# Slot 0 of the second mixture set between the last steps of the states' block, token sums fixed behind their slot, and a second staging buffer for weights

## The chip, the cores and the metric

The kernel runs on one core of a Trainium2 chip. The core has TensorE (PE, matrix products into PSUM), VectorE (DVE), ScalarE (ACT), GpSimd (POOL, here only an issuer of transfers) and SyncE (SP, the other issuer). Each engine works through its own queue in order, and waits by semaphores for the others. The metric is the device time of one execution in microseconds: 1490.43 as the median of three runs (1489.2 to 1496.42).

## The reference, cut to what matters

```
attention:  x (8, 8, 512, 64), state (8, 8, 32, 64), scale 1/8
  a     = softmax(scale * x @ state^T)      xread = a  @ state
  a2    = softmax(scale * state @ x^T)      sread = a2 @ x
  out   = concat([xread, sread], axis=2)    -> 8 x (512 + 32) = 4352 rows of 512
mixture 1 (d_ff 1536):  x = ((x @ w_a) * (x @ w_b)) @ w_out
mixture 2 (d_ff 2048):  h = x @ w_in;  x = (h - tanh(h)) @ w_out
```

All is float32. The kernel writes each operand of a large product as a high and a low part (a rounded copy and what is left), and multiplies hi·hi + hi·lo + lo·hi, so that every product is three matmuls. Weights come as 64-bit floats and are decoded on the chip.

## The kernel before, in words

**Blocks.** The 4352 rows are taken as nine blocks with the model's 512 features on partitions: eight of 512 tokens (one for each batch) and a last one, `blk == NB`, of 256 columns, the states. Attention of a block runs beside the first mixture of the block before.

**First mixture.** A block has `FA = 12` steps, one for each 128 of d_ff. `AB(blk, f)` computes the two products into the PSUM banks p2 and p3 (`pab`); ACT copies the first (`ac`), DVE multiplies it by the second, ACT and DVE split the result into `ph` (L517 to L520). `X1(blk, f - 1)` adds the output product of the step before to the four banks `acc`; after step 11 the banks are copied to `ev` and stored to a buffer `x1d` in memory (L535 to L540).

**Weights of the second mixture.** Beside token blocks 2, 3, 5, 6 and 7, `b_words` decodes the second mixture's weights. For `w_in` it also forms the sums and differences of 256-column pieces that Strassen's scheme (in Winograd's form) needs. Each result is split on ACT and DVE into one staging buffer, `hlb` in the place w22, and POOL stores it to memory: `whd` for `w_in` (two stores for each buffer), `wod` for `w_out`. They are loaded again as `wh` and `wo` when they are used.

**Second mixture.** It runs in slots. A slot `(blk, j)` is one eighth of d_ff for one block; `slots` lists all 72. For a token block, `pair_slot` forms 256 rows of h for 512 columns by seven half-sized products, the *pieces*, each a `part` of six matmuls: the token operands are B11, B21, B22 and the sums T1 to T4, made of the block's `x1r` and `x1s` (two halves of the block, loaded by `xr_load`) in seven stages of `x_stage` (L567 to L575). Products gather in the PSUM tiles px, py and pz; px is copied between its pieces (`snap`, L682, L695, L701, L712) and DVE adds the copies to py and pz to get h (L691, L704, L715). From h, ACT and DVE make g = h − tanh(h) (a polynomial where h is small) with u, t, y, k, then `g` as high and low parts. g of slot s goes into the output product `O` (matmuls `acc<-g,wo`) during slots s + 1 and s + 2. The states' block takes the plain form of the slot.

**What sets the order.** The program is written in one order; a scheduler then places every instruction in its engine's queue, by that order and by when it thinks operands are there. So an instruction can stand well ahead of its place in the program. A pool of buffers gives names in turn; an instruction that fills a buffer waits for the last reader of what was in it. `tc.issue_after(x)` keeps what is inside from being placed ahead of x.

**The passage.** The code from L880 on runs the states' block through its twelve steps; step 3 ends with the load of block 0, steps 5 to 11 each hold one stage of its sums. Slot 0 begins behind that, with the last output product of the states' block (`X1(NB, FA - 1)`) between its first pieces:

```
        if f == 3:
            xr_load(0, 5)
        if 4 < f:
            x_stage(0, f - 5)
...
        if blk < NB:
            pair_slot(s, between=(lambda: X1(NB, FA - 1)) if s == 0 else None)
```

Of the kernel before, what the change touches and what calls it, by code (L numbers as in the profile page):

```python
# [8 lines left out]
F32 = mybir.dt.float32  # L9
# [7 lines left out]
KT = 4  # L17
FA = 12
# [26 lines left out]
def fused_kernel(ctx: ExitStack, tc, xT, xn, stp, stq, wA, wB, outT, outS):  # L45
# [153 lines left out]
    half = slice(0, 256), slice(256, 512)  # L199
    U = {}  # L200

    def keep(src, to):
        hl = w_tile(22, [128, 2, 2, 256], F32R, "hlb")
        s3 = src.rearrange("p (a c) -> p a c", a=2)
        nc.scalar.mul(hl[:, :, 0, :], s3, 2.0 ** -8)  # L205
        nc.vector.scalar_tensor_tensor(hl[:, :, 1, :], s3, 2.0 ** -8, hl[:, :, 0, :].bitcast(F32),  # L206
                                       ALU.mult, ALU.subtract)
        for i, d in enumerate(to):
            nc.gpsimd.dma_start(d, hl[:, i].rearrange("p h c -> p (h c)"))

    def b_words():
        i = BU[0]
        BU[0] += 1
        j, part = divmod(i, 6)
        d = whd[j]
        if part in (0, 1, 4, 5):
            raw = DB.raw.pop(0)
            t = small.get([128, 512], I32, "bt", DT)
            h = raw[:, :, 1]
            nc.scalar.mul(h.bitcast(F32), h.bitcast(F32), 2.0 ** -111)  # L220
            words(t, h, raw)
            DB.done += 1
            if DB.done not in (11, 12):
                DB.load()
            t = t.bitcast(F32)
            if part < 2:
                U[part] = t
                keep(t, [d[:, 1], d[:, 2]] if part == 0 else [d[:, 0], d[:, 7]])
            else:
                f = j + FP * (part - 4)  # L230
                hl = w_tile(22, [128, 2, 512], F32R, "hlb")
# [11 lines left out]
    BU = [0]  # L243

    def wh_load(s, j, nb=False):

# [253 lines left out]
    def AB(blk, f, bg=None, after=None):  # L500
        n = 512 if blk < NB else 256
        a = None
        for s in range(2):
            pt = ab.get([128, 512], F32, "pab")
            if blk < NB:
                m = MM[blk, f].rearrange("p a (g s c) -> p a g s c", g=2, s=2)
                for G in range(2):
                    product(pt, (m[:, 0, G, s, :], m[:, 1, G, s, :]), HL[blk][G], slice(0, n), G == 0, G == 1)
            else:
                for k in range(KT):  # L510
                    product(pt, [w[:, s, k, :] for w in WH[f]], X0S[k], slice(0, n), k == 0, k == KT - 1)
            if s == 0:
                a = small.get([128, 512], F32, "ac", AC)
# [12 lines left out]
    def X1(blk, f):  # L526
# [5 lines left out]
            product(acc[m], pair(WO[f], block(m)), ph, slice(0, n), f == 0, f == FA - 1)  # L532
        if f == FA - 1:
            for m in range(KT):
                e = small.get([128, 512], F32, "ev", AT) if m < 3 else small.get([128, 512], F32, "ev", AC)  # L535
                if m % 2:
                    nc.vector.tensor_copy(e[:, :n], acc[m][:, :n])
                else:
# [14 lines left out]
    def width(s):  # L553
        return 512 if slots[s][0] < NB else 256

    def xr_load(blk, place):
        n = 512 if blk < NB else 256
        raw = [big.get([128, 2, 512], F32, "x1r", XIN), w_tile(place, [128, 2, 512], F32, "x1s")]
        for m in range(KT):
            nc.sync.dma_start(raw[m // 2][:, m % 2, :n], x1d[blk][m])  # L560
        RAWX[blk] = raw
        XB[blk] = {}

    def x_pair(blk, name, i, src):
# [64 lines left out]
        nc.vector.copy_predicated(y, k.bitcast(I32), t)  # L629

    def g_hi(s, g):
        GG[s, g] = big.get([128, 2, 512], F32R, "g", Q[0:3] + mix.names[0:2])
        nc.scalar.copy(GG[s, g][:, 0, : width(s)], EW[s, g][2])  # L633

    def g_lo(s, g):
# [29 lines left out]
        O(s, g, m)  # L665
        evac(s, g, m)

    def pair_slot(s, between=None):
        blk, j = slots[s]
        y_, z_ = (abp.tile([128, 512], F32, tag=t, name=n)[:, half[0]] for t, n in (("p0", "py"), ("p2", "pz")))  # L670
# [5 lines left out]
        if between:  # L676
            between()
        if s:
            dve_rest(s - 1, 0)
            act_ut(s - 1, 1)  # L680
# [12 lines left out]
            dve_rest(s - 1, 1)  # L693
        part(x_, s, 3, "T2", False, True)
        nc.scalar.copy(sn[:, 1], x_)  # L695
        part(z_, s, 4, "T3", True, True)
        OE(s - 2, 1, 2)
        part(x_, s, 5, "T1", False, True)
        nxt = border.index(blk) + 1
        stage = {0: 0}.get(j, j - 1 if j > 1 else None)  # L700
        nc.scalar.copy(sn[:, 2], x_)  # L701
        if s:
            g_hi(s - 1, 1)
        nc.vector.tensor_tensor(h2[:, half[1]], sn[:, 2], z_, ALU.add)  # L704
        if s:
            g_lo(s - 1, 1)
        OE(s - 2, 1, 3)
        O(s - 1, 0, 0)
        if stage is not None and nxt < len(border):
            x_stage(border[nxt], stage)  # L710
        part(x_, s, 6, "B22", False, True)
        nc.scalar.copy(h1[:, half[1]], x_)  # L712
        O(s - 1, 0, 1)
        part(z_, s, 7, "T4", False, True)
        nc.vector.tensor_tensor(h2[:, half[0]], sn[:, 1], z_, ALU.add)  # L715
# [161 lines left out]
                t()  # L877


    for f in range(FA):  # L880
        AB(NB, f)
# [6 lines left out]
        if f > 0:  # L888
            X1(NB, f - 1)
        else:  # L890
            X1(NB - 1, FA - 1)
        if f >= 4 and 2 * f - 1 in OPL:
            wo_load(OPL.index(2 * f - 1))
        if f == 3:
            xr_load(0, 5)
        if 4 < f:
            x_stage(0, f - 5)

    last = len(slots) - 1
    for s, (blk, j) in enumerate(slots):  # L900
        if j == 0 and blk < NB:
            xr_load(blk + 1, 21)
        if blk < NB:
            pair_slot(s, between=(lambda: X1(NB, FA - 1)) if s == 0 else None)
        else:
            plain_slot(s)
        if s < last - 1:
# [54 lines left out]
```

## Time and profile before

| | |
|---|---|
| median of three runs | 1490.43 us (1489.2 to 1496.42) |
| the profiled execution | 1493.69 us |
| its span, first to last instruction | 1491.6 us |
| mean granted clock of TensorE, share of full | 0.995 |
| busy PE, PE weight loads, DVE, ACT, POOL | 98%, 82%, 75%, 60%, 11% |
| chain that ended last | PE 80%, DMA 8%, DVE 6%, issue 4%, ACT 2% |

The span is the time between the first and the last instruction; the profiled execution's own time has some 2 us around it. Matmuls are pipelined and their ends are modelled, so PE counts as busy also when it works slowly: the clock stands beside it. The granted clock has two levels here, 2.4 GHz (1.00) and 1.2 GHz (0.50); a stretch with both shows their mean. Along the time, the first 60 us hold the start, attention and first mixture run to about 690 us, the states' block to about 753 us, the second mixture to the end.

### The profile page before, as it was taken

The page shows a single profiled execution, that of the slowest core. Times are in us where ns is not written, and L with a number is a line of the kernel's source. Part 1 is how long each engine was busy: PE and PEld are TensorE (multiplying, and loading weights), DVE is VectorE, ACT ScalarE, POOL GpSimd, SP SyncE. Part 2 cuts the span into 40 slices and gives each one's busy share as a digit, 9 for nine tenths or more (in the row PEclk, how much of TensorE's full clock was granted, in tenths as well). Part 3 has the DMA queues.
Part 4 walks back from the last instruction along what each step waited for, and adds up shares of the span by engine and source line. Part 5 has one row for each costly group of instructions (what it writes and reads, how often), then busy time and mean ns, then how long its engine had stood idle before and what let it go on. Part 6 is the DMA issues. An engine that isn't in the chain of part 4 may idle for free.

```text
span 1491.6 us, 23237 instructions
## 1 busy us (share of the span) xinstructions
PE 1461.5 (98%) x8660; PEld 1225.8 (82%) x8660; DVE 1122.7 (75%) x1969; ACT 894.6 (60%) x1721; POOL 168.6 (11%) x318
## 2 busy tenths in 40 slices
PE   6999999999999999999899999999999999999999
PEld 3776777777888777788888888888888889888998
DVE  6986645777543768674378989889898988888887
ACT  5764445555443555453266867777676777777665
POOL 0000001222000222220210000000000010001010
PEclk9999999999999999999999999999999999999999
DMA  8733435676456576753875655756565665756544
GB/s 288 244 124 115 151 125 188 214 222 209 128 138 178 160 242 212 224 188 116 264 228 176 223 177 175 227 177 223 179 224 177 185 218 170 219 169 205 170 142 127
DMA packets 102624, 280.44 MB, mean 188 GB/s; under 512 B 14064, under 2 KB 43248, under 8 KB 92784
## 3 DMA queue, kind: packets, MB, share of 16 engines
q0 software_dynamic: 40320, 178.28, 39.2%
q1 hardware_dynamic: 62192, 100.68, 20.4%
q8 instruction: 68, 1.11, 0.3%
q14 instruction: 44, 0.36, 0.1%
HBM read 216.53 MB, written 62.39 MB: 187 GB/s over the span
## 4 chain that ended last, share of the span: by engine, by line
PE 80%; DMA 8%; DVE 6%; issue 4%; ACT 2%; POOL 1%; SPq 0%; ACTq 0%; POOLq 0%; DVEq 0%
PE acc L417 37%; PE pab L417 13%; PE px L598 12%; PE pz L598 6%; DMA whd<-hlb 4%; PE py L598 3%; PE mq L471 3%; PE mp L430 2%; DMA wod<-hlb 1%; DVE hlb L206 1%; ACT hlb L205 1%; DMA x1s<-x1d 1%; PE sc L292 1%; DVE ph L520 1%; PE pr L367 1%
## 5 line engine op out<-in xcount | busy, mean ns | idle before, releaser
L417 PE MATMUL acc<-g,wo 128*128 128x512 f32 (+1 forms) x1728 | 438.2, 386 | 0.1
L417 PEld LDWEIGHTS acc<-g,wo 128*128 128x128 f32 x1728 | 293.0, 190 | 42.9 <-DVE g L638 2.4
L417 PE MATMUL acc<-ph,wo 128*128 128x512 f32 (+1 forms) x1296 | 307.8, 385 | 7.7 <-DVE ph L520 4.8
L417 PE MATMUL pab<-hl,mx 128*128 128x512 f32 x1152 | 294.6, 403 | 1.5 <-ACT ac L514 1.5
L417 PEld LDWEIGHTS acc<-ph,wo 128*128 128x128 f32 x1296 | 232.8, 189 | 61.0 <-DVE ph L520 5.5
L417 PEld LDWEIGHTS pab<-hl,mx 128*128 128x128 f32 x1152 | 212.5, 189 | 63.8 <-issue 9.1
L249 POOL DMA_DIRECT2D wh<-whd x144 | 76.2, 529 | 678.7 <-PE pz L598 608.3
L517 DVE TENSOR_TENSOR ac<-ac,pab 128x512 f32<-128x512 f32 (+1 forms) x108 | 70.5, 652 | 109.3 <-PE pab L417 108.3
L633 ACT CAST g<-y 128x512 fp32r<-128x512 f32 (+1 forms) x144 | 85.7, 595 | 89.8 <-DVE y L629 89.1
L598 PEld LDWEIGHTS px<-T,wh 128*128 128x128 f32 x768 | 108.3, 190 | 15.4 <-ACT snap L695 2.6
L598 PE MATMUL px<-T,wh 128*128 128x256 f32 x768 | 114.7, 286 | 3.4 <-ACT snap L695 1.8
L638 DVE TENSOR_TENSOR g<-y,g 128x512 fp32r<-128x512 f32 (+1 forms) x144 | 95.1, 660 | 26.9 <-ACT g L633 26.9
L598 PE MATMUL px<-B,wh 128*128 128x256 f32 x768 | 115.1, 285 | 0.0
L598 PE MATMUL pz<-T,wh 128*128 128x256 f32 x768 | 114.7, 283 | 0.0
L598 PEld LDWEIGHTS pz<-T,wh 128*128 128x128 f32 x768 | 106.8, 190 | 6.9
L598 PEld LDWEIGHTS px<-B,wh 128*128 128x128 f32 x768 | 106.3, 192 | 6.7 <-ACT snap L701 0.5
L622 DVE SCALAR_TENSOR_TENSOR y<-y,u 128x512 f32<-128x512 f32 (+1 forms) x144 | 95.0, 660 | 20.0 <-ACT y L614 18.9
L629 DVE COPY_PREDICATED y<-k,t 128x512 f32<-128x512 int32 (+1 forms) x144 | 104.4, 725 | 2.1
L514 ACT COPY ac<-pab 128x512 f32<-128x512 f32 (+1 forms) x108 | 60.1, 557 | 72.5 <-PE pab L417 70.9
L618 ACT ACTIVATE k<-u,consts 128x512 f32<-128x512 f32 (+1 forms) x144 | 99.8, 693 | 0.0
L623 DVE SCALAR_TENSOR_TENSOR u<-t,u 128x512 f32<-128x512 f32 (+1 forms) x144 | 94.3, 655 | 7.1 <-ACT k L618 1.0
L614 ACT ACTIVATE y<-u,consts 128x512 f32<-128x512 f32 (+1 forms) x144 | 99.0, 688 | 0.7 <-DVE g L638 0.6
(234 smaller groups left out, 2059.2 us busy)
## 6 DMA issues: line engine op xcount, KB each, us to landing
wh<-whd POOLq DMA_DIRECT2D x64, 1024.0 KB, 5.3
wh<-whd POOLq DMA_DIRECT2D x72, 768.0 KB, 4.6
ml<-md POOLq DMA_DIRECT2D x72, 256.0 KB, 3.3
raw<-in_wB SPq DMA_DIRECT2D x32, 512.0 KB, 4.6
whd<-hlb POOLq DMA_DIRECT2D x64, 256.0 KB, 3.1
rawab<-in_wA SPq DMA_DIRECT2D x12, 1024.0 KB, 5.4
md<-mst SPq DMA_DIRECT2D x48, 256.0 KB, 2.5
x1d<-ev SPq DMA_DIRECT2D x32, 256.0 KB, 3.8
```

Source lines behind the costliest of these rows:

```text
L249: nc.gpsimd.dma_start(t.rearrange("p a h c -> p a (h c)"), whd[j][:, a:b])
L417: nc.tensor.matmul(dst[:, cols], w[a], x[:, c, cols], start=first and i == 0, stop=last and i == 2)
L514: nc.scalar.copy(a[:, :n], pt[:, :n])
L517: at_v = nc.vector.tensor_tensor(a[:, :n], a[:, :n], pt[:, :n], ALU.mult)
L598: nc.tensor.matmul(dst, WP[s, piece][:, a, block(k)], XB[slots[s][0]][x][:, c, k, :], start=first and k == 0 and i == 0, stop=last and k = ...
L614: nc.scalar.activation(y, u, AF.Square, bias=consts[:, 0:1], scale=1.0)
L618: nc.scalar.activation(k, u, AF.Relu, bias=consts[:, 1:2], scale=1.0)
L622: nc.vector.scalar_tensor_tensor(y, y, PK, u, ALU.add, ALU.mult)
L623: nc.vector.scalar_tensor_tensor(u, t, C3, u, ALU.mult, ALU.mult)
L629: nc.vector.copy_predicated(y, k.bitcast(I32), t)
L633: nc.scalar.copy(GG[s, g][:, 0, : width(s)], EW[s, g][2])
L638: nc.vector.tensor_tensor(gt[:, 1, :n], EW.pop((s, g))[2], gt[:, 0, :n].bitcast(F32), ALU.subtract)
```

## The change

The edit has four parts.

- `stage()` gives the staging buffer of the weights: by turns the place w22 and a place m3 out of `mix`, which at other times holds the states' `sq` and the slots' `snap`.
- Slot 0 is taken out of the loop over slots. `pair_slot` becomes a generator that stops (`yield`) at five points, and the loop over the steps of the states' block drives it during steps 9, 10 and 11. Its pz lies in bank p0, since p2 and p3 are in use by `pab`. Block 0 is loaded in halves behind steps 1 and 3, its seven stages follow the products of steps 4 to 7, and the last output product of the states' block moves behind the first two pieces of slot 1.
- In the states' block `ac` and the four `ev` go to the two RAW places q4 and q5 (`ev` had five places in AT and AC, `ac` two in AC), so that the places of u, t, y, k are free for slot 0. The turn of the places for `g` begins at q2.
- `x_stage` in a slot is held behind the third copy of px and the sum that reads it (`issue_after`). In block 0 the stages of block 1 lie in slots 1 to 7, in later blocks in slots 0 and 2 to 7.

```
--- before.py
+++ after.py
@@ -199,8 +199,15 @@
     half = slice(0, 256), slice(256, 512)
     U = {}
 
+    def stage():
+
+        BU[1] += 1
+        if BU[1] % 2:
+            return w_tile(22, [128, 2, 512], F32R, "hlb")
+        return mix.get([128, 2, 512], F32R, "hlb", SQ)
+
     def keep(src, to):
-        hl = w_tile(22, [128, 2, 2, 256], F32R, "hlb")
+        hl = stage().rearrange("p h (a c) -> p (h a c)", a=2).rearrange("p (a h c) -> p a h c", a=2, h=2)
         s3 = src.rearrange("p (a c) -> p a c", a=2)
         nc.scalar.mul(hl[:, :, 0, :], s3, 2.0 ** -8)
         nc.vector.scalar_tensor_tensor(hl[:, :, 1, :], s3, 2.0 ** -8, hl[:, :, 0, :].bitcast(F32),
@@ -228,7 +235,7 @@
                 keep(t, [d[:, 1], d[:, 2]] if part == 0 else [d[:, 0], d[:, 7]])
             else:
                 f = j + FP * (part - 4)
-                hl = w_tile(22, [128, 2, 512], F32R, "hlb")
+                hl = stage()
                 split(hl, t)
                 nc.gpsimd.dma_start(wod[f], flat(hl))
         elif part == 2:
@@ -240,7 +247,7 @@
             nc.vector.tensor_tensor(U[0][:, half[1]], U[0][:, half[1]], U[0][:, half[0]], ALU.subtract)
             keep(U[0], [d[:, 3], d[:, 6]])
 
-    BU = [0]
+    BU = [0, 0]
 
     def wh_load(s, j, nb=False):
 
@@ -510,7 +517,7 @@
                 for k in range(KT):
                     product(pt, [w[:, s, k, :] for w in WH[f]], X0S[k], slice(0, n), k == 0, k == KT - 1)
             if s == 0:
-                a = small.get([128, 512], F32, "ac", AC)
+                a = small.get([128, 512], F32, "ac", AC) if blk < NB else big.get([128, 512], F32, "ac", RAW)
                 nc.scalar.copy(a[:, :n], pt[:, :n])
         if bg:
             bg()
@@ -532,7 +539,10 @@
             product(acc[m], pair(WO[f], block(m)), ph, slice(0, n), f == 0, f == FA - 1)
         if f == FA - 1:
             for m in range(KT):
-                e = small.get([128, 512], F32, "ev", AT) if m < 3 else small.get([128, 512], F32, "ev", AC)
+                if blk == NB:
+                    e = big.get([128, 512], F32, "ev", RAW)
+                else:
+                    e = small.get([128, 512], F32, "ev", AT if m < 3 else AC)
                 if m % 2:
                     nc.vector.tensor_copy(e[:, :n], acc[m][:, :n])
                 else:
@@ -553,12 +563,13 @@
     def width(s):
         return 512 if slots[s][0] < NB else 256
 
-    def xr_load(blk, place):
+    def xr_load(blk, place, parts=(0, 1)):
         n = 512 if blk < NB else 256
-        raw = [big.get([128, 2, 512], F32, "x1r", XIN), w_tile(place, [128, 2, 512], F32, "x1s")]
-        for m in range(KT):
-            nc.sync.dma_start(raw[m // 2][:, m % 2, :n], x1d[blk][m])
-        RAWX[blk] = raw
+        for i in parts:
+            t = w_tile(place, [128, 2, 512], F32, "x1s") if i else big.get([128, 2, 512], F32, "x1r", XIN)
+            for m in range(2):
+                nc.sync.dma_start(t[:, m, :n], x1d[blk][2 * i + m])
+            RAWX.setdefault(blk, []).append(t)
         XB[blk] = {}
 
     def x_pair(blk, name, i, src):
@@ -629,7 +640,7 @@
         nc.vector.copy_predicated(y, k.bitcast(I32), t)
 
     def g_hi(s, g):
-        GG[s, g] = big.get([128, 2, 512], F32R, "g", Q[0:3] + mix.names[0:2])
+        GG[s, g] = big.get([128, 2, 512], F32R, "g", Q[2:3] + mix.names[0:2] + Q[0:2])
         nc.scalar.copy(GG[s, g][:, 0, : width(s)], EW[s, g][2])
 
     def g_lo(s, g):
@@ -665,16 +676,16 @@
         O(s, g, m)
         evac(s, g, m)
 
-    def pair_slot(s, between=None):
+    def pair_slot(s):
+
         blk, j = slots[s]
-        y_, z_ = (abp.tile([128, 512], F32, tag=t, name=n)[:, half[0]] for t, n in (("p0", "py"), ("p2", "pz")))
+        y_ = abp.tile([128, 512], F32, tag="p0", name="py")[:, half[0]]
         x_ = abp.tile([128, 512], F32, tag=f"p{1 + 2 * (s % 2)}", name="px")[:, half[0]]
         sn = mix.get([128, 3, 256], F32, "snap", SQ)
         h1, h2 = (mix.get([128, 512], F32, "h", [nm]) for nm in (mix.names[2], "ml2"))
         part(y_, s, 2, "B21", True, True)
         part(x_, s, 1, "B11", True, True)
-        if between:
-            between()
+        yield
         if s:
             dve_rest(s - 1, 0)
             act_ut(s - 1, 1)
@@ -693,23 +704,28 @@
             dve_rest(s - 1, 1)
         part(x_, s, 3, "T2", False, True)
         nc.scalar.copy(sn[:, 1], x_)
+        z_ = abp.tile([128, 512], F32, tag="p2" if s else "p0", name="pz")[:, half[0]]
         part(z_, s, 4, "T3", True, True)
+        yield
         OE(s - 2, 1, 2)
         part(x_, s, 5, "T1", False, True)
+        yield
         nxt = border.index(blk) + 1
-        stage = {0: 0}.get(j, j - 1 if j > 1 else None)
-        nc.scalar.copy(sn[:, 2], x_)
+        stage = j - 1 if j > 1 or blk == 0 else (0, None)[j]
+        at_s = nc.scalar.copy(sn[:, 2], x_)
         if s:
             g_hi(s - 1, 1)
-        nc.vector.tensor_tensor(h2[:, half[1]], sn[:, 2], z_, ALU.add)
+        at_v = nc.vector.tensor_tensor(h2[:, half[1]], sn[:, 2], z_, ALU.add)
         if s:
             g_lo(s - 1, 1)
         OE(s - 2, 1, 3)
         O(s - 1, 0, 0)
-        if stage is not None and nxt < len(border):
-            x_stage(border[nxt], stage)
+        if stage not in (None, -1) and nxt < len(border):
+            with tc.issue_after(at_s.ins), tc.issue_after(at_v.ins):
+                x_stage(border[nxt], stage)
         part(x_, s, 6, "B22", False, True)
         nc.scalar.copy(h1[:, half[1]], x_)
+        yield
         O(s - 1, 0, 1)
         part(z_, s, 7, "T4", False, True)
         nc.vector.tensor_tensor(h2[:, half[0]], sn[:, 1], z_, ALU.add)
@@ -877,31 +893,39 @@
                 t()
 
 
+
+    slot = pair_slot(0)
     for f in range(FA):
-        AB(NB, f)
+        stages = {4: (0,), 5: (1, 2), 6: (3, 4), 7: (5, 6)}.get(f, ())
+        AB(NB, f, after=lambda: [x_stage(0, i) for i in stages])
         if f == 0:
             wo_load(0)
         if f in (3, 7):
             wh_load(f // 4, f // 4)
         if f >= 4 and 2 * f - 2 in OPL:
             wo_load(OPL.index(2 * f - 2))
-        if f > 0:
-            X1(NB, f - 1)
-        else:
-            X1(NB - 1, FA - 1)
+        if f >= 9:
+            next(slot, None)
+        X1(*((NB, f - 1) if f else (NB - 1, FA - 1)))
+        if f in (9, 10):
+            next(slot)
         if f >= 4 and 2 * f - 1 in OPL:
             wo_load(OPL.index(2 * f - 1))
-        if f == 3:
-            xr_load(0, 5)
-        if 4 < f:
-            x_stage(0, f - 5)
+        if f in (1, 3):
+            xr_load(0, 5, (f // 2,))
+    xr_load(1, 21)
+    wh_load(2, slots[2][1])
 
     last = len(slots) - 1
     for s, (blk, j) in enumerate(slots):
+        if s == 0:
+            continue
         if j == 0 and blk < NB:
             xr_load(blk + 1, 21)
         if blk < NB:
-            pair_slot(s, between=(lambda: X1(NB, FA - 1)) if s == 0 else None)
+            for i, _ in enumerate(pair_slot(s)):
+                if s == 1 and i == 0:
+                    X1(NB, FA - 1)
         else:
             plain_slot(s)
         if s < last - 1:
```

How the queues stand. First DVE in the states' block before, between the `ph` of two steps (ac and ph are the product and its low part; L575 is a subtraction among the token sums, x1r the first half of a block's load):

```order
L520 TENSOR_TENSOR ph<-ac,ph 128x256
L569 TENSOR_TENSOR T_6975<-x1s,T_6975 128x512
L517 TENSOR_TENSOR ac<-ac,pab 128x256
L575 TENSOR_TENSOR x1r<-x1r 128x2x256
L520 TENSOR_TENSOR ph<-ac,ph 128x256
L517 TENSOR_TENSOR ac<-ac,pab 128x256
```

The same queue in the change, around the stages of steps 6 and 7:

```order
L524 TENSOR_TENSOR ac<-ac,pab 128x256
L586 TENSOR_TENSOR x1r<-x1s,x1r 128x2x256
L527 TENSOR_TENSOR ph<-ac,ph 128x256
L580 TENSOR_TENSOR T_6707<-x1r,T_6707 128x512
L580 TENSOR_TENSOR T_6711<-x1s,T_6711 128x512
L524 TENSOR_TENSOR ac<-ac,pab 128x256
L527 TENSOR_TENSOR ph<-ac,ph 128x256
```

The subtraction for block 1 no longer stands among the steps of the states' block; the sums of block 0 stand behind `ph` of their step.

PE at the end of the states' block before (acc<-ph is the output product of a step, px, py and pz are pieces of slots; wo_1061 and wo_1114 belong to steps 10 and 11):

```order
L417 MATMUL acc<-ph,wo_1061 128x256 x12
L598 MATMUL py<-B_6771,wh_6545 128x256 x6
L598 MATMUL px<-B_6663,wh_6545 128x256 x6
L417 MATMUL acc<-ph,wo_1114 128x256 x12
L598 MATMUL px<-T_6875,wh_6545 128x256 x6
L598 MATMUL pz<-T_6926,wh_6545 128x256 x6
L598 MATMUL px<-T_6823,wh_6547 128x256 x6
L598 MATMUL py<-B_6771,wh_6751 128x256 x4
L598 MATMUL px<-B_6715,wh_6547 128x256 x6
```

And in the change, from output 10 on (wh_6550 is slot 0, wh_6768 and wh_6770 are slot 1, acc<-g the token outputs of slot 0):

```order
L609 MATMUL pz<-T_6765,wh_6550 128x256 x6
L424 MATMUL acc<-ph,wo_1061 128x256 x12
L609 MATMUL py<-B_6655,wh_6768 128x256 x6
L609 MATMUL px<-B_6599,wh_6768 128x256 x6
L424 MATMUL acc<-ph,wo_1114 128x256 x12
L609 MATMUL px<-T_6711,wh_6768 128x256 x6
L609 MATMUL pz<-T_6762,wh_6768 128x256 x6
L609 MATMUL px<-T_6707,wh_6770 128x256 x6
L424 MATMUL acc<-g,wo_0_6395 128x512 x3
L609 MATMUL px<-B_6651,wh_6770 128x256 x6
L424 MATMUL acc<-g,wo_0_6395 128x512 x3
L609 MATMUL pz<-T_6765,wh_6770 128x256 x6
```

Slot 0 is through before output 10, and slot 1 stands where slot 0 stood, with token outputs between its pieces.

ACT in the change at the same place (u, t, y, k of slot 0's second half, then two of the four `ev` among the px copies of slot 1):

```order
L620 ACTIVATE u<-h 128x512
L621 ACTIVATE t<-h 128x512
L625 ACTIVATE y<-u,consts 128x512
L629 ACTIVATE k<-u,consts 128x512
L549 COPY ev<-acc 128x256
L693 COPY snap<-px 128x256
L644 CAST g<-y 128x512
L706 COPY snap<-px 128x256
L549 COPY ev<-acc 128x256
L715 COPY snap<-px 128x256
L578 CAST B_7144<-x1r 128x512
```

Before, the two copies `ev<-acc` stood together behind the first px copy of slot 0.

## Rows read from the trace of the kernel before

**Rows 1.** The page, busy time of each engine (us, share, instructions).
```profile
PE 1461.5 (98%) x8660; PEld 1225.8 (82%) x8660; DVE 1122.7 (75%) x1969; ACT 894.6 (60%) x1721; POOL 168.6 (11%) x318
```

**Rows 2.** Stretches: busy us of each engine (instructions), granted clock, DMA share, GB/s.
```profile
630.00:640.00 10.00, 8.81 (x31) 7.06 (x32) 8.63 (x15) 4.93 (x9) 2.88 (x5) 0.83 0.64 215
...
720.00:730.00 10.00, 5.61 (x45) 5.40 (x44) 2.56 (x6) 0.98 (x3) 2.12 (x4) 0.85 1.02 346
730.00:740.00 10.00, 10.00 (x72) 10.00 (x71) 1.27 (x3) 1.36 (x4) 1.58 (x3) 0.81 0.54 162
...
760.00:770.00 10.00, 7.92 (x42) 6.80 (x41) 9.00 (x16) 7.63 (x16) 0.60 (x2) 0.83 0.67 208
...
800.00:1490.00 690.00, 688.04 (x4329) 618.75 (x4327) 602.58 (x1064) 494.64 (x995) 69.32 (x131) 1.00 0.61 188
```

**Rows 3.** Timeline of PE: start, us, line, operation, out<-in, count [idle before <-releaser].
```profile
710.50 1.58 PE L417 MATMUL acc<-ph,wo 128*128 128x256 f32 x12
...
729.49 2.72 PE L417 MATMUL acc<-ph,wo 128*128 128x256 f32 x11 [4.39 <-DVE ph L520]
...
770.44 0.88 PE L598 MATMUL pz<-T,wh 128*128 128x256 f32 x6
...
823.79 0.88 PE L598 MATMUL py<-B,wh 128*128 128x256 f32 x6
...
825.23 1.57 PE L417 MATMUL acc<-g,wo 128*128 128x512 f32 x6
826.63 0.88 PE L598 MATMUL px<-T,wh 128*128 128x256 f32 x6
```

**Rows 4.** Timeline of DVE, same columns: the passage, and a later slot.
```profile
728.41 0.69 DVE L575 TENSOR_TENSOR x1r<-x1r 128x512 f32<-128x512 f32 x1 [7.20 <-DMA x1r<-x1d]
...
821.00 0.69 DVE L638 TENSOR_TENSOR g<-y,g 128x512 fp32r<-128x512 f32 x1 [0.39 <-ACT g L633]
822.59 0.42 DVE L715 TENSOR_TENSOR h<-snap,pz 128x256 f32<-128x256 f32 x1 [0.89 <-PE pz L598]
823.37 0.69 DVE L622 SCALAR_TENSOR_TENSOR y<-y,u 128x512 f32<-128x512 f32 x1 [0.36 <-ACT y L614]
```

**Rows 5.** Chain of work that ended last, 700 to 775 us: start, us, what.
```profile
703.48 2.88 PE pab L417 x24
...
706.36 1.43 PE acc L417 x12
...
708.17 6.03 DMA x1s<-x1d
```

**Rows 6.** Waits of ACT, 240 to 690 us: total us, times, longest.
```profile
ACT hlb L205 <- DMA whd<-hlb: 57.2, 19, 5.4
```

**Rows 7.** Timeline of ACT: the token blocks' last part, and slots 0 and 1.
```profile
617.44 0.63 ACT L205 ACTIVATE hlb<-bt 128x512 fp32r<-128x512 f32 x1 [5.35 <-DMA whd<-hlb]
...
751.99 0.37 ACT L539 COPY ev<-acc 128x256 f32<-128x256 f32 x1
...
758.62 0.63 ACT L609 ACTIVATE u<-h 128x512 f32<-128x512 f32 x1
...
760.91 0.61 ACT L609 ACTIVATE u<-h 128x512 f32<-128x512 f32 x1
```

**Rows 8.** Waits of PE, 240 to 690 us: total us, times, longest.
```profile
PE acc L417 <- DVE ev L537: 2.6, 2, 1.9
PE pab L417 <- ACT ac L514: 1.5, 2, 1.1
PE pt L303 <- ACT S L350: 1.4, 2, 0.8
```

**Rows 9.** The tile hlb: from issue to landing of its stores.
```profile
DMA to landing us min/median/max: 2.3/3.1/6.2
```

**Rows 10.** DMA issues: count, KB each, median us to landing.
```profile
x1d<-ev SPq DMA_DIRECT2D x4, 128.0 KB, 2.5
```

**Rows 11.** The buffer x1d in memory: from issue to landing, all sizes.
```profile
DMA to landing us min/median/max: 2.0/4.2/8.0
```

More of the change, by code (lines that the diff above doesn't have):

```diff
@@ L200, in fused_kernel, with stage @@
     U = {}
+    def stage():
+        BU[1] += 1
+        if BU[1] % 2:
+            return w_tile(22, [128, 2, 512], F32R, "hlb")
+        return mix.get([128, 2, 512], F32R, "hlb", SQ)
     def keep(src, to):
-        hl = w_tile(22, [128, 2, 2, 256], F32R, "hlb")
+        hl = stage().rearrange("p h (a c) -> p (h a c)", a=2).rearrange("p (a h c) -> p a h c", a=2, h=2)
         s3 = src.rearrange("p (a c) -> p a c", a=2)
@@ L230, in b_words @@
                 f = j + FP * (part - 4)
-                hl = w_tile(22, [128, 2, 512], F32R, "hlb")
+                hl = stage()
                 split(hl, t)
@@ L534, in X1 @@
             for m in range(KT):
[L535 removed]
+                if blk == NB:
+                    e = big.get([128, 512], F32, "ev", RAW)
+                else:
+                    e = small.get([128, 512], F32, "ev", AT if m < 3 else AC)
                 if m % 2:
@@ L554, in width, with xr_load @@
         return 512 if slots[s][0] < NB else 256
-    def xr_load(blk, place):
+    def xr_load(blk, place, parts=(0, 1)):
         n = 512 if blk < NB else 256
[L558 to L561, printed above, removed]
+        for i in parts:
+            t = w_tile(place, [128, 2, 512], F32, "x1s") if i else big.get([128, 2, 512], F32, "x1r", XIN)
+            for m in range(2):
+                nc.sync.dma_start(t[:, m, :n], x1d[blk][2 * i + m])
+            RAWX.setdefault(blk, []).append(t)
         XB[blk] = {}
@@ L666, in OE, with pair_slot @@
         evac(s, g, m)
-    def pair_slot(s, between=None):
+    def pair_slot(s):
         blk, j = slots[s]
-        y_, z_ = (abp.tile([128, 512], F32, tag=t, name=n)[:, half[0]] for t, n in (("p0", "py"), ("p2", "pz")))
+        y_ = abp.tile([128, 512], F32, tag="p0", name="py")[:, half[0]]
         x_ = abp.tile([128, 512], F32, tag=f"p{1 + 2 * (s % 2)}", name="px")[:, half[0]]
@@ L675, in pair_slot @@
         part(x_, s, 1, "B11", True, True)
-        if between:
-            between()
+        yield
         if s:
@@ L695, in pair_slot @@
         nc.scalar.copy(sn[:, 1], x_)
+        z_ = abp.tile([128, 512], F32, tag="p2" if s else "p0", name="pz")[:, half[0]]
         part(z_, s, 4, "T3", True, True)
+        yield
         OE(s - 2, 1, 2)
         part(x_, s, 5, "T1", False, True)
+        yield
         nxt = border.index(blk) + 1
-        stage = {0: 0}.get(j, j - 1 if j > 1 else None)
-        nc.scalar.copy(sn[:, 2], x_)
+        stage = j - 1 if j > 1 or blk == 0 else (0, None)[j]
+        at_s = nc.scalar.copy(sn[:, 2], x_)
         if s:
             g_hi(s - 1, 1)
-        nc.vector.tensor_tensor(h2[:, half[1]], sn[:, 2], z_, ALU.add)
+        at_v = nc.vector.tensor_tensor(h2[:, half[1]], sn[:, 2], z_, ALU.add)
         if s:
@@ L708, in pair_slot @@
         O(s - 1, 0, 0)
-        if stage is not None and nxt < len(border):
-            x_stage(border[nxt], stage)
+        if stage not in (None, -1) and nxt < len(border):
+            with tc.issue_after(at_s.ins), tc.issue_after(at_v.ins):
+                x_stage(border[nxt], stage)
         part(x_, s, 6, "B22", False, True)
         nc.scalar.copy(h1[:, half[1]], x_)
+        yield
         O(s - 1, 0, 1)
@@ L877, in fused_kernel @@
                 t()
+    slot = pair_slot(0)
     for f in range(FA):
-        AB(NB, f)
+        stages = {4: (0,), 5: (1, 2), 6: (3, 4), 7: (5, 6)}.get(f, ())
+        AB(NB, f, after=lambda: [x_stage(0, i) for i in stages])
         if f == 0:
@@ L887, in fused_kernel @@
             wo_load(OPL.index(2 * f - 2))
[L888 to L891, printed above, removed]
+        if f >= 9:
+            next(slot, None)
+        X1(*((NB, f - 1) if f else (NB - 1, FA - 1)))
+        if f in (9, 10):
+            next(slot)
         if f >= 4 and 2 * f - 1 in OPL:
             wo_load(OPL.index(2 * f - 1))
[L894 to L897, printed above, removed]
+        if f in (1, 3):
+            xr_load(0, 5, (f // 2,))
+    xr_load(1, 21)
+    wh_load(2, slots[2][1])
     last = len(slots) - 1
     for s, (blk, j) in enumerate(slots):
+        if s == 0:
+            continue
         if j == 0 and blk < NB:
@@ L903, in fused_kernel @@
         if blk < NB:
-            pair_slot(s, between=(lambda: X1(NB, FA - 1)) if s == 0 else None)
+            for i, _ in enumerate(pair_slot(s)):
+                if s == 1 and i == 0:
+                    X1(NB, FA - 1)
         else:
```

6 lines of the change are left out of this document (3 added, 3 removed).

## The prediction

> **What bounds the kernel now.** I read the page first: TensorE (PE) has matmuls for 98% of the span [rows 1], so only time in which PE stands still or runs slowly can be won. The table of stretches shows where that is. From 800 us to the end PE is idle for 690 − 688.04 = 1.96 us in all, so the second mixture, once it runs, has nothing to give [rows 2]. The losses lie in two places.
>
> The first is the passage from the states' block into the second mixture, 710 to 771 us. The timeline of PE shows a stop of 4.39 us before 729.49, put down to the product `ph` of VectorE (DVE) [rows 3]. The timeline of DVE shows the reason: a subtraction for the *second* block's token sums (L575) stood ahead of `ph` in DVE's queue and waited 7.20 us for its load x1r [rows 4]. The granted clock falls during the stop, and again later: 0.85, 0.81 and 0.83 over the windows 720 to 730, 730 to 740 and 760 to 770 [rows 2], that is 3.0 + 3.8 + 3.4 = 10.2 us at the lower of the two levels, 1.2 GHz.
>
> What the passage loses is best told by its work. One step of the states' block is 24 matmuls of the two products (2.88 us, all 24 in the chain's row) and 12 of the output (1.41) [rows 5]; two of the seven pieces of a slot are 825.23 − 823.79 = 1.44, one is 0.72, and 6 token matmuls are 826.63 − 825.23 = 1.40 [rows 3]. Between the start of the output of step 3 (710.50) and the end of the T4 piece of slot 1 (770.44 + 0.72 = 771.16) PE did 7 x 2.88 + 9 x 1.41 of the states' block, the 14 pieces of slots 0 and 1 and 7 matmuls ahead out of slot 2 (15.17 x 0.72), and 12 token matmuls (2.80): 20.2 + 12.7 + 10.9 + 2.8 = 46.6 us of work in 60.7. **14.1 us** are lost there.
>
> By PE's busy column the loss would be smaller: 4.39 us idle in 720 to 730, none in 730 to 740, 2.08 in 760 to 770 [rows 2], 6.5 in all. The Trainium skill ("Perfetto Trace Analysis", Identifying the Most-Contended Engine) says that matmul busy share is no good measure for TensorE. The trace agrees: 730 to 740 is 10.00 us busy at a clock of 0.81. By the busy column the passage could give 6.5 us, by its work 14.1.
>
> The second place is the preparation of the second mixture's weights beside the token blocks. ScalarE (ACT) waits there 57.2 us, in 19 waits, for the store of the one staging buffer `hlb` [rows 6], up to 5.35 us at a time [rows 7], and its copies out of PSUM stand behind it. PE feels four of these waits: 2.6 us in two through `ev` and 1.5 in two through `ac` [rows 8]. Around the last of them the clock is 0.83 over 10 us [rows 2]: 3.4 us at 1.2 GHz, 1.7 lost. Together **5.8 us**.
>
> **The change part by part.** *Two staging buffers.* The store of a buffer lands 2.3 to 6.2 us after its issue, median 3.1 [rows 9]. A step of a token block has 24 matmuls of 512 columns, 24 x 1.40/6 = 5.6 us [rows 3], and one buffer is filled in a step. With the second buffer ACT returns to a buffer after two steps, 11.2 us, so even the slowest store is in. I take 5.8 us. It adds no instruction. Bounds: 0, if ACT then waits for something as late; a little below nothing, −1.4, if ACT's shifted order doubles the wait of `pt` on `S`, which the change doesn't touch [rows 8]; above, 5.8.
>
> *Slot 0 between steps 9 to 11, the sums of block 0 in steps 4 to 7.* The matmuls are the same. I laid out PE's new order by hand from 710.50 with the durations above. To the end of the products of step 9: 5 x 1.41 + 5 x 2.88, 732.0. From there two pieces, output 8, T2 and T3, products 10, T1, output 9, B22, products 11, T4, output 10, two pieces of slot 1, output 11: 9 x 0.72 + 4 x 1.41 + 2 x 2.88 = 17.9, end 749.8. Then T2, T3, T1, three token matmuls, B22, three, T4, six: 5 x 0.72 + 2.8 = 6.4, end 756.2 without a wait. Against it stands 771.16 less the 7 matmuls of slot 2 (0.84): 770.3.
>
> T3 of slot 0 now shares a bank of PSUM with py and waits for the sum that reads it; output 8 (1.41) lies between and covers the copy (0.37 [rows 7]) and the sum. Two waits are new. (a) PE's T2 of slot 1 needs the copy of px, and ACT has it behind u, t, y, k of slot 0's second half, which begin when T4's sum is there, on DVE behind the last `ph`, at about 747. The four take 760.91 − 758.62 = 2.29 us, the `ev` and the px copy after them 0.37 each [rows 7]: px is out at 750.1 to 750.4, and PE waits 0.5. (b) `ev` of the states' block has two buffers in place of four. The third `ev` waits on ACT for the first one's store, and behind it on ACT is the third copy of px, on which B22 waits; the fourth does the same on DVE, with T4 behind its sum. The first `ev` ends at 749.8; four such stores landed a median of 2.5 us after issue [rows 10], so the third `ev` starts at 752.3 and px is out at 753.1, when PE has just come to B22 (749.8 + 0.5 + 2.16 + 0.70 = 753.2). I put down 0.5 us for what passes between engines. Transfers to and from that memory at large took 2.0 to 8.0 [rows 11]; with 2.0 the wait is gone, with 8.0 it is 757.8 + 0.7 − 753.2 = 5.3. I take the 2.5, as it is the same store. So the end is 756.2 + 1.0 = 757.2 and the passage gains **13.1 us**, between 14.1 (no wait) and 14.1 − 0.5 − 5.3 − 1.7 (one more spell at 1.2 GHz like that after the `ev` stop) = 6.6.
>
> Block 0's second load x1s doesn't move: 6.03 us from 708.17 [rows 5], in at 714.2. The order now puts its first reader behind `ph` of step 5, whose products end at 710.50 + 1.41 + 2.88 = 714.8, so it costs nothing. The loads of block 1 and the weights of slot 2 go out earlier on SP and POOL; what stands behind them there, the last weights of the second mixture, is read by slots much later.
>
> *Token sums behind their slot.* No instruction more, but a fixed place: one cast on ACT and up to two DVE instructions (some 1.3 us) in each of 51 slots, after the third px copy and its sum, where before they were bunched early in a block. In a slot without them DVE has three waits of 0.39, 0.89 and 0.36 us just there, 1.64 in all [rows 4], and the `g` that comes later by it is ready at 821.7 and first read at 825.23 [rows 3]. So it fits: nothing. Bounds: 1.96 us gained [rows 2]; lost, up to the instructions' own time, see the last rival.
>
> **The sum.** 13.1 + 5.8 = 18.9 us from the profiled execution's 1493.69 (span 1491.6 and 2.1 around it): 1474.8. The median of the runs, 1490.43, is 3.3 below that execution, so I predict 1490.43 − 18.9 = 1471.5, **1472 us**.
>
> **The rivals.** *The store of the first `ev` decides* (ACT and DVE at the end of the states' block). For it: SP issues it just after the loads of block 1, and landings up to 8.0 are in the trace. Against: the median of this very store. At 8.0 us with a spell at 1.2 GHz the passage gains 6.6: 1478.0. *The staging gains nothing.* For it: the stores get slower, or ACT's stop is only handed to the next late operand. Against it: 11.2 us for at most 6.2. The gain is 13.1: 1477.3. The Trainium skill ("SBUF — State Buffer", SBUF: two separate sides) warns that a transfer issued by POOL gets no descriptors while DVE runs an instruction that takes both read ports. By that rule these stores land later the busier DVE gets, and a second buffer would only move the wait; the landings reach 6.2 us, twice the median, but no row says in which mode DVE ran. *Slower: the pinned sums hold up each slot.* If DVE can't use its idle time because a sum's operand or the next px copy comes in its middle, `g` and h of each slot come late and PE waits in 51 slots. At 18.9/51 = 0.37 us a slot the gain is gone, from 0.52 the kernel is slower by more than 0.5%; at 0.63, one ACT instruction over 512 columns [rows 7], it costs 32 us, 1504. Against it: 1.64 us idle for 1.3 of work, and 3.5 us between `g` and its reader.
>
> **How the numbers follow.** Forecast 0.64, late store 0.17, staging without gain 0.13, slower 0.04, and 0.02 for pinned sums that eat between half and all of the gain. The lowest time that the bounds allow is 1490.4 − 14.1 − 5.8 − 2.0 = 1468.5; the runs here lie down to 1.2 below their median, so 1467. Upward, the first two rivals together give 1483.8; I stop at 1482 and leave out the slow case. A measurement of this kernel can tell some 0.5%, 7.5 us, from no change: faster means below 1483. The forecast and nearly all of the first two rivals are: faster 0.90; the worst of them and half-eaten gains: same 0.07; slower 0.03.
>
> **What would show it.** Right: no stop of PE above 1 us between 710 and 760, T4 of slot 1 done near 757, the granted clock 1.00 in both places, next to no wait of ACT for stores of `hlb`, 800 us to the end unchanged in length. Wrong: a wait of ACT of several us for a store at the third `ev`; waits of PE on `g` or px copies that recur in every slot; ACT's stops before `hlb` still there with another releaser.

## The result, and the profile after

The changed kernel took 1471.15 us (median of four runs, 1470.33 to 1472.2). The kernel before, on the same chip, took 1491.95 (four runs, 1489.2 to 1496.42). The ratio is 0.9858 with a 95% interval of [0.9831, 0.9885]. The forecast was 1472. The profiled execution took 1472.2 us, with a span of 1470.4, 21.2 less than before.

The page, first the busy time of each engine, then the shares of the chain that ended last:

```profile
PE 1451.6 (99%) x8660; PEld 1223.9 (83%) x8660; DVE 1128.3 (77%) x1969; ACT 904.4 (62%) x1721; POOL 167.6 (11%) x318
...
PE 96%; DMA 1%; DVE 1%; ACT 1%; issue 0%; SPq 0%; ACTq 0%; DVEq 0%
```

The chain has become PE's: 96% after 80%. PE's busy time fell by 1461.5 − 1451.6 = 9.9 us [rows 1] and its idle time by the other 11.3. So nearly half of the gain was time in which PE counted as busy and worked slowly or with small gaps, and the idle time alone doesn't tell the loss. I take it as in the prediction, by its work: for every matmul, the distance to the start of the next one over the usual distance for its shape, summed by stretch (times of the kernel before):

| stretch | lost before | lost after | gain | forecast |
|---|---|---|---|---|
| start, to 60 us | 16.8 | 16.4 | 0.4 | 0 |
| token blocks, 240 to 690 | 12.7 | 4.5 | 8.2 | 5.8 |
| passage, 690 to 800 | 14.1 | 4.4 | 9.7 | 13.1 |
| second mixture, from 800 | 3.3 | 0.4 | 2.9 | 0 |

The sum is 21.2, the difference of the spans (from 60 to 240 us both kernels lose the same); 18.9 were forecast. Three of the four terms missed by 2.4 to 3.4 us, and the misses nearly cancel. The same stretches as in [rows 2], in the changed kernel:

```profile
630.00:640.00 10.00, 10.00 (x44) 8.08 (x44) 7.25 (x13) 4.82 (x9) 2.63 (x5) 1.00 0.63 217
...
720.00:730.00 10.00, 10.00 (x86) 10.00 (x85) 1.69 (x4) 2.30 (x6) 2.50 (x5) 1.00 1.00 351
730.00:740.00 10.00, 10.00 (x86) 10.00 (x86) 5.05 (x11) 5.60 (x12) 2.12 (x4) 1.00 0.85 272
740.00:750.00 10.00, 7.15 (x45) 6.48 (x44) 7.25 (x14) 4.86 (x12) 0.53 (x1) 0.87 0.88 284
750.00:760.00 10.00, 10.00 (x62) 8.97 (x62) 8.26 (x15) 6.39 (x14) 1.06 (x2) 0.96 0.41 111
```

At 630 and at 720 to 740 the clock is 1.00 and PE has work throughout: 86 matmuls in 720 to 730 where there were 45. One loss is left, at 740 to 760. The timeline of PE there (columns as in [rows 3]), then ACT, then the queue of SP:

```profile
742.99 0.89 PE L609 MATMUL px<-T,wh 128*128 128x256 f32 x6
743.72 0.85 PE L424 MATMUL acc<-g,wo 128*128 128x512 f32 x3
747.42 1.65 PE L609 MATMUL px<-B,wh 128*128 128x256 f32 x6 [2.85 <-ACT snap L715]
748.87 1.48 PE L424 MATMUL acc<-g,wo 128*128 128x512 f32 x3
750.15 1.15 PE L609 MATMUL pz<-T,wh 128*128 128x256 f32 x6
```

```profile
740.79 0.35 ACT L549 COPY ev<-acc 128x256 f32<-128x256 f32 x1
...
742.48 0.37 ACT L706 COPY snap<-px 128x256 f32<-128x256 f32 x1 [0.54 <-PE px L609]
746.72 0.37 ACT L549 COPY ev<-acc 128x256 f32<-128x256 f32 x1 [3.87 <-DMA x1d<-ev]
746.99 0.38 ACT L715 COPY snap<-px 128x256 f32<-128x256 f32 x1
```

```profile
738.84 0.80 SPq L571 DMA_DIRECT2D x1s<-x1d  x2
741.17 7.24 SPq L550 DMA_DIRECT2D x1d<-ev  x4
```

This is wait (b) of the prediction. The first `ev` ends at 741.14; the third, in the same buffer, starts 5.58 us later, when the store has landed; behind it stands the third px copy, and for that PE waits 2.85 us before B22. Then 12 matmuls start at the lower clock, the first piece taking 1.65 instead of 0.88: (0.13 + 0.04) x 10 = 1.7 us at full speed lost by the two windows.

ACT's waits in 240:690 (total us, times, longest), the longest group and the two longest before `hlb`, and then the landing of `hlb`:

```profile
ACT ac L521 <- PE pab L424: 47.5, 42, 2.8
...
ACT hlb L212 <- issue: 12.1, 7, 1.8
ACT hlb L212 <- DVE bt L243: 10.4, 8, 1.3
```

```profile
DMA to landing us min/median/max: 2.3/3.8/6.6
```

The 57.2 us of [rows 6] are gone altogether, and so are 18.3 us in eight waits for the stores to `wod` that those rows leave out, though the stores land later than before (median 3.8, 3.1 in [rows 9]): two steps of 5.6 us still cover the longest.

The second mixture's gain is in no wait of PE. The starts of `py`, the first piece of a slot, over a block's edge in the kernel before, and in the changed one:

```profile
834.43 0.88 PE L598 MATMUL py<-B,wh 128*128 128x256 f32 x6
845.20 0.88 PE L598 MATMUL py<-B,wh 128*128 128x256 f32 x6
856.08 0.88 PE L598 MATMUL py<-B,wh 128*128 128x256 f32 x6
866.88 0.88 PE L598 MATMUL py<-B,wh 128*128 128x256 f32 x6
877.52 0.88 PE L598 MATMUL py<-B,wh 128*128 128x256 f32 x6
```

```profile
816.38 0.88 PE L609 MATMUL py<-B,wh 128*128 128x256 f32 x6
827.01 0.88 PE L609 MATMUL py<-B,wh 128*128 128x256 f32 x6
837.65 0.88 PE L609 MATMUL py<-B,wh 128*128 128x256 f32 x6
848.29 0.88 PE L609 MATMUL py<-B,wh 128*128 128x256 f32 x6
```

Before, three slots at each block's edge took 10.77, 10.88 and 10.80 us, the others 10.64; after, all take 10.64. What stretched them stands in the waits of the *weight loads* (PEld), 800:1490, before and then after:

```profile
PEld acc L417 <- DVE g L638: 2.4, 7, 0.4
PEld acc L417 <- ACT g L633: 1.3, 6, 0.2
```

```profile
PEld acc L424 <- DVE g L649: 0.3, 1, 0.3
```

Where the sums were bunched, early in a block, `g` came late: 3.7 us in 13 waits, 0.3 now. They are too short to show as idle time of a pipelined PE.

### The profile page after: what moved, and what is told of

It is laid out like the page before. It is cut to its first block, busy times and chain, and to the rows that moved or that the text cites. A ratio compares the mean times of both kernels' runs of the same rounds, so it can differ in the third digit from the quotient of the medians.

```text
span 1470.4 us, 23250 instructions
## 1 busy us (share of the span) xinstructions
PE 1451.6 (99%) x8660; PEld 1223.9 (83%) x8660; DVE 1128.3 (77%) x1969; ACT 904.4 (62%) x1721; POOL 167.6 (11%) x318
## 4 chain that ended last, share of the span: by engine, by line
PE 96%; DMA 1%; DVE 1%; ACT 1%; issue 0%; SPq 0%; ACTq 0%; DVEq 0%
PE acc L424 45%; PE pab L424 21%; PE px L609 12%; PE pz L609 6%; PE py L609 3%; PE mq L478 3%; PE mp L437 2%; PE pr L374 1%; PE sc L299 1%; DMA x1d<-ev 1%; DMA rawab<-in_wA 1%; PE pt L310 0%; PE mp L443 0%; PE pa L310 0%; DVE sm L324 0%
```

## The experiments

Two questions were open: what made the store behind wait (b) late, and which part of the change earned what. Edits marked "after" start from the changed kernel, "before" from the other. The kernel before ran beside each of them; its medians were 1491.95 to 1492.83, and as the runs are from several chips, a difference of 1 us between two kernels isn't counted.

**The ev wait by more buffers** (after; the four `ev` two to a buffer, so that none waits for a store):

```
 if blk == NB:
-    e = big.get([128, 512], F32, "ev", RAW)
+    if m % 2 == 0:
+        pair_ev = big.get([128, 2, 512], F32, "ev", RAW)
+    e = pair_ev[:, m % 2]
```

> The changed kernel with one edit: the four ev of the states' block lie two to a buffer (as the token blocks' ev do), so that no ev waits for a store. Theory A (the stop of 2.85 us of PE before B22 of slot 1, and the half-speed stretch behind it, come from the third ev's wait for the first one's store): the stop and the low clock at 744 to 751 us go, 3 to 4.4 us less than the changed kernel, 1467 to 1468 us, ratio to before 0.984. Rival (ACT's and DVE's queues are late there anyway, the store is only the last of several): a stop of 2 us or more stays with another releaser, time 1470 to 1471.5.

(The token blocks' `ev` in fact lie one to a buffer; nothing rests on that remark.)

1466.41 us (1465.6 to 1466.89), ratio 0.9827 [0.9807, 0.9848]. The stop is gone, and with it the lower clock:

```profile
740.00:750.00 10.00, 10.00 (x69) 9.00 (x68) 9.79 (x18) 7.50 (x16) 1.05 (x2) 1.00 0.89 302
```

So wait (b) with its spell at the lower clock cost 1471.15 − 1466.41 = 4.7 us, where 0.5 had been put down.

**The ev wait by an earlier landing** (after; still two buffers, but block 1's second load goes out behind the stores; `STORE` keeps the last store of `ev`):

```
-xr_load(1, 21)
+xr_load(1, 21, (0,))
...
 X1(NB, FA - 1)
+with tc.issue_after(STORE[0].ins):
+    xr_load(1, 21, (1,))
```

> The changed kernel with one transfer moved: the second load of block 1 (x1s, 2 x 256 KB) is issued on SP behind the four stores of ev of the states' block, not just ahead of them; the ev keep their two buffers. In the changed kernel SP issues x1s at 738.84 and it lands 7.0 us later (median of two), the first ev's store is issued at 741.17, and the third ev starts at 746.72. Theory Q (the store lands late because it shares its queue and its engines with the 512 KB of x1s just ahead of it): without them it lands in about the 2.5 us of the kernel before; the third ev then waits under 1.0 us on ACT, the stop of PE of 2.85 us falls under 0.6 with no spell at 1.2 GHz behind it, and the time is 1466 to 1467.5, as with the four ev in two buffers (1466.4). Theory G (what is late is the general load of weights, wh and wo on POOL's queue, in flight at the same time): the store still lands after 4.5 to 6 us, the stop stays at 2 to 3 us and the time at 1470 to 1472. In between (landing 3.5 to 4): both share in it, stop near 1.0 to 1.5, 1467.5 to 1469.5. Neither theory expects a wait on x1s itself, which is first read in slot 2.

1466.59 us (1465.89 to 1467.19), ratio 0.9819 [0.9792, 0.9846]. ACT, then the queue of SP:

```profile
739.98 0.35 ACT L551 COPY ev<-acc 128x256 f32<-128x256 f32 x1
...
742.50 0.38 ACT L551 COPY ev<-acc 128x256 f32<-128x256 f32 x1 [0.46 <-DMA x1d<-ev]
```

```profile
740.36 4.57 SPq L552 DMA_DIRECT2D x1d<-ev  x4
745.02 1.21 SPq L573 DMA_DIRECT2D x1s<-x1d  x2
```

The store is in 2.17 us after the first `ev` ended, the wait is 0.46, and PE doesn't stop. So it was x1s, ahead of the store in SP's queue, that made it late, as theory Q has it. But x1s stood as far ahead of the store in the kernel before. What differs is how long x1s itself took (count, KB each, median us to landing; before, then the change):

```profile
x1s<-x1d SPq DMA_DIRECT2D x2, 256.0 KB, 4.0
```

```profile
x1s<-x1d SPq DMA_DIRECT2D x2, 256.0 KB, 7.0
```

In both kernels the first store landed 0.3 us behind x1s: at 755.1 after 754.8, and at 746.6 after 746.3. Whether the place in the queue made it wait, or the 512 KB more on the same DMA engines, these runs don't separate. Nor is theory G refuted. The 768 KB of weights went out on POOL as before (at 736.99), but the 1024 KB only when the first store had landed; in the change they were under way during the wait (issued at 743.56). And in this run the fourth store of `ev`, issued at 744.61 with no load of SP left ahead of it, took 5.5 us where the three before it had taken 1.7 to 2.1. It landed 0.4 us behind these 1024 KB:

```profile
742.75 0.53 POOL L256 DMA_DIRECT2D wh<-whd  x1 [5.24 <-PE pz L611]
```

```profile
x1d<-ev SPq DMA_DIRECT2D x1, 128.0 KB, 5.5
```

The Trainium skill ("DMA: Bandwidth & Descriptors", Queues, rings and completion order) says that what SP issues goes into one queue, consumed in order on each DMA engine, and that an engine alternates between queues. The trace agrees: a store with x1s ahead in SP's queue landed just behind it, and of two stores with only POOL's weights ahead one took 2.1 us and one 5.5.

**The weights behind the stores as well** (the kernel above, `wh_load(2, ...)` moved into the same `with`).

> As the kernel with x1s issued behind the ev stores, and the weight loads of slot 2 (wh, 1024 and 768 KB on POOL, in the changed kernel at 728.46 and 737.80) written behind them as well. Only the landing of the first ev's store tells here; the time may suffer from weights that come late. Theory Q (x1s ahead in the same queue makes the store late): the store lands as in the kernel with x1s alone moved, 2.2 to 3 us, and these weights change nothing but their own lateness: slot 2, which starts near 750, waits for wh some 0 to 5 us, time 1466 to 1474. Theory G (the weights in flight make it late): here alone the store lands in 2.0 to 3 us, while with x1s alone moved it took 4.5 to 6.

1466.61 us (1466.05 to 1467.8), ratio 0.9821 [0.9791, 0.9851]. The edit moved nothing: holding orders the program, but makes POOL wait for nothing on SP, and POOL's queue stood as before. It repeats the run above, and is no test of its own for the weights, which were never moved.

**Staging alone** (before, with `stage()` as in the change).

> The kernel before with the second staging buffer alone. Theory A (the parts add up; the token blocks gain by this buffer alone what they gained in the changed kernel): ACT's waits for stores of hlb go, PE's stops at 305, 317, 617 and 629 us go; 8 us less than before, about 1484 us; the stop of 4.39 us at 725 us is still there. By the sum of the prediction: 5.8 us less, 1486. Rival (the waits move to another operand): within 1.5 us of before.

1484.84 us (1477.77 to 1485.65), ratio 0.994 [0.9918, 0.9962]: 7.8 us gained against the 1492.65 beside it. The loss in the token blocks falls from 12.7 to 4.0, and the passage keeps its stop; on DVE its cause stands as in [rows 4]:

```profile
717.95 0.69 DVE L582 TENSOR_TENSOR x1r<-x1r 128x512 f32<-128x512 f32 x1 [6.63 <-DMA x1r<-x1d]
```

**One staging buffer** (after, `if BU[1] % 2:` made `if True:`).

> The changed kernel with one staging buffer again, all else kept. Theory A (the parts add up): ACT's waits for stores are back, 57 us in the token blocks, and with them 8 us: 1479 us, 12.5 us less than before. Rival (the passage and the staging share a cause, as by the scheduler's order): 1475 or less, or 1484 or more.

1477.21 us (1473.66 to 1478.85), ratio 0.9897 [0.9872, 0.9922], 6.1 above the changed kernel. Waits of PE in 240:690 (total us, times, longest):

```profile
PE acc L424 <- DVE ev L547: 3.0, 2, 1.9
PE pab L424 <- ACT ac L521: 1.4, 1, 1.4
PE pt L310 <- ACT S L357: 1.0, 2, 0.8
```

All three groups of [rows 8], of which the changed kernel has none, are back, the waits of `pt` on `S` among them, which the prediction had called untouched.

**Holding the token sums alone** (before; slot 0 stays where it was, one staging buffer):

```
-            x_stage(border[nxt], stage)
+            with tc.issue_after(at_s.ins), tc.issue_after(at_v.ins):
+                x_stage(border[nxt], stage)
```

> The kernel before with the token sums held behind the third px copy and its sum (issue_after) and nothing else: slot 0 stays behind the states' block. Theory B (most of the passage's loss came from the subtraction for block 1 that stood ahead of ph on DVE): the stop of 4.39 us goes, with its 3.4 us of clock loss; the second mixture is 3 us faster as in the changed kernel; 8 to 11 us less than before, 1481 to 1484. Theory C (the passage's loss is the chain of px copies, sums, u, t, y, k to g of slots 0 and 1 with nothing to do on PE meanwhile, and only work between the steps fills it): the stop moves into slots 0 and 1, the gain is 3 to 5 us, 1487 to 1489.

1479.38 us (1477.54 to 1482.42), ratio 0.9917 [0.9892, 0.9942]: 13.3 gained, more than expected by either. The waits of PE in the passage (690:800) are now:

```profile
PE px L598 <- ACT t L610: 1.5, 1, 1.5
PE px L598 <- ACT snap L695: 0.5, 1, 0.5
PE acc L417 <- DVE ph L520: 0.4, 1, 0.4
```

The stop of 4.39 us on `ph` is gone, since block 1's subtraction can no longer stand ahead of it; the loss of the passage is 4.2 us after 14.1, and from 800 us on every slot but one takes 10.64. So 9.9 of the 13.3 us lie in the passage, and about 3 in the second mixture.

**Staging and holding, slot 0 not moved** (before, with both edits above).

> The kernel before with the second staging buffer and the held token sums, and without the move of slot 0 (no slot between the steps of the states' block, ev in four buffers). Theory B (the held sums gave most of the passage, staging and sums add up): 13.3 us by the sums as run alone plus 8 by staging, 1492 - 21 = 1470 to 1472, as fast as the changed kernel; so the move as made, with its wait for the store of ev, is worth nothing. Rival (the two overlap, the move is needed): 1475 or more.

1471.5 us (1470.98 to 1474.53), ratio 0.9865 [0.9842, 0.9888]: the changed kernel's time, without the move. The two gains add up: 7.8 + 13.3 = 21.1, measured 1492.62 − 1471.5 = 21.1.

**The change without holding** (after, `x_stage` in a slot without its `with`).

> The changed kernel with the token sums of the slots no longer held behind their px copy; the move of slot 0, its stages and the second staging buffer are kept. Theory B (the holding is what keeps block 1's subtraction away from ph on DVE and makes slots even): the 3 us of the second mixture are lost again, slots at a block's edge take 10.8 us and not 10.64, and DVE waits for x1r or x1s ahead of a sum that PE waits for; 1476 to 1482. Rival (the move alone is enough, as block 1's first load comes 20 us earlier in it): the passage is as in the changed kernel, only the 3 us are lost, 1474.

1478.38 us (1478.08 to 1478.84), ratio 0.9907 [0.9882, 0.9931], as theory B had it. Slots at a block's edge take 10.76 to 10.88 again, and in the passage PE waits 3.3 and 2.6 us for px copies.

**The same with ev in pairs.**

> The same without holding, with the four ev two to a buffer as in the fastest version (1466.4). It tells whether what the move and the holding take away in the passage is the same loss. Rival of B (the move alone is enough): passage free of stops, the second mixture 3 us longer, 1469.5. Theory B (a load of block 1 still stops DVE in front of a sum): a stop of PE of 2 us or more between 735 and 760 us, 1472 to 1476.

1477.41 us (1476.92 to 1478.47), ratio 0.9901 [0.988, 0.9922], 11.0 above the kernel with ev pairs and holding. Its DVE, its ACT and its PE:

```profile
726.21 0.69 DVE L588 TENSOR_TENSOR x1r<-x1r 128x512 f32<-128x512 f32 x1 [6.22 <-DMA x1r<-x1d]
```

```profile
726.98 0.62 ACT L580 CAST T<-x1r 128x512 fp32r<-128x512 f32 x1 [5.10 <-DVE x1r L588]
```

```profile
728.23 0.98 PE L611 MATMUL px<-T,wh 128*128 128x256 f32 x6 [2.51 <-ACT snap L695]
```

Block 1's subtraction stands among the steps of the states' block again. Now a cast on ACT waits for it, and slot 0's px copies, which stand behind that cast, come late. The stop lies earlier than theory B had it, and the time is above its range. The move alone doesn't keep the subtraction out; the holding does. All kernels with two staging buffers, in us:

| | sums not held | sums held |
|---|---|---|
| slot 0 not moved | 1484.84 | 1471.5 |
| slot 0 moved, `ev` waits | 1478.38 | 1471.15 |
| slot 0 moved, `ev` free | 1477.41 | 1466.41 |

By the sum over matmuls the passage loses some 15.5, 9.0 and 7.4 us in the three kernels of the first column, and 4.5, 4.4 and nothing in those of the second. So the two parts overlap. With the sums held, the move is worth 0.35 us as it was made (intervals overlap), and 5.1 once `ev` is free; without, 1484.84 − 1478.38 = 6.5. The holding is worth 13.3 without the move, 7.2 with it and 11.0 once `ev` is free.

## Why the prediction was right, and where it wasn't

- **What bounds the kernel, and the total.** Right in the main: 17.9 of the 21.2 us came out of the two places that it named. The other 2.9 came from the second mixture, which it had left out, and 0.4 from the start. Counting by work (14.1 us) and not by the busy column was needed: 9.7 came out of the passage, and 14.1 in the kernel with `ev` in pairs, which loses nothing there. The busy column's 6.5 was too low even as idle time: the windows 710 to 720 and 750 to 760, which the prediction left out, hold 0.67 and 1.31 us more, 8.45 in all.
- **Wait (b), put down at 0.5.** This is the step that failed. The chain of the wait was right, and so was its formula: with the measured 5.58 us in place of 2.5 it gives 749.8 + 5.58 + 0.7 − 753.2 = 2.9, and 2.85 was measured. The landing was mis-sized. I took [rows 10] "as it is the same store", but in both kernels that store lands just behind x1s, which SP issues 2.2 to 2.3 us ahead of it; before, x1s landed in 4.0 us, in the change in 7.0. The runs show that without x1s ahead the store is in after 2.17. Why x1s itself took longer is not tested; 512 and 768 KB of weights went out on POOL at 737.08 and 737.80, just ahead of it. The rival of the late store named the place and the reason, at 8.0 us; the truth lay between the two.
- **The spell at the lower clock** behind that wait, in the bounds at 1.7 and in the forecast at nothing, came. Stop and clock together are 4.4, where 1.0 was forecast for both waits: the whole miss of the passage. Wait (a) does not show.
- **Token sums, held at nothing.** Too small, and the larger part booked elsewhere. From 800 us on they gave 2.9, above the bound of 1.96: the prediction took PE's idle time ("nothing to give") as the bound, by the busy column that it had warned against two paragraphs later. And the passage's gain, booked under slot 0 and its stages, comes by the holding alone: it leaves 4.2 of 14.1 us lost, where the move alone leaves 9.0 of 15.5 (with two staging buffers). The order of DVE's queue told it, for the subtraction that waited 7.20 us was one of block 1's, and it is the holding that keeps those out; the move touches block 0's.
- **Staging, 5.8.** Right in mechanism, too small: 7.8 alone, 6.1 when taken out of the change, 8.2 by the stretch. The waits of `pt` on `S` (1.4) hung on it too: they went with the second buffer and came back with the single one. The rest, about 1 us, are gaps too short for a row of the waits. The stated upper bound of 5.8 was none, since it counted only the stops put down to `ev` and `ac`, and the clock.
- **The rivals.** Neither staging that gains nothing nor pinned sums that cost came true. The stores of `hlb` landed later (3.8 after 3.1) and the time didn't feel it; no run tells why they did.
- **The signs.** Of those that were to show it right, the end of ACT's waits for stores of `hlb` came. There was a stop of PE above 1 us, the clock in the passage fell below 1.00, and the second mixture got shorter. The first sign of being wrong, a wait of ACT of several us at the third `ev`, was there (3.87).

So the total was right partly by luck: +2.4 and +2.9 (and 0.4 at the start) against −3.4. The chances stood on mechanisms, two of which had their sizes or their owner wrong.

## What to carry to other kernels

When an in-order queue stops on an operand that comes from memory, look whether the stopped instruction belongs there at all: here the sums of block 1, placed too early by the scheduler, cost some 10 us in the passage, and holding them back gave these without moving slot 0. When buffers are taken away, size the new wait by the transfers that will be under way when its own goes out (here x1s, itself late), not by the same transfer elsewhere. And bound a steady loop by its period against its own best period (10.64 here), not by the idle time of a pipelined engine.

## What was not expected of the hardware

- Two loads of 256 KB issued 2.3 us ahead in the same queue moved a 128 KB store from 2.17 to 5.58 us (from the end of the copy to the start of the next in its buffer). In the kernel before, the same loads stood 2.2 us ahead, and the store landed 2.7 us after its issue.
- Beside 1024 KB of POOL's weights, issued 1.9 us ahead, such a store took 5.5 us with no load ahead of it in SP's queue.
- Three slots at a block's edge ran 0.13 to 0.24 us long with PE counted as busy throughout; only the weight loads' waits (up to 0.4 us each) showed it.
- The granted clock fell to the 1.2 GHz level behind a stop of 2.85 us (0.87 and 0.96 over the two windows); in the kernels with `ev` in pairs or with x1s moved, which don't have that stop, it was 1.00 at the same place.
